# Paired PV matmuls on two banks, and MoE2's second weight factored one phase later

## The chip, the cores and the metric

The kernel runs on one core of a Trainium2 chip. The metric is the device time of one execution in microseconds (us), and lower is better. TensorE (PE in the profile) does the matmuls, VectorE (DVE) and ScalarE (ACT) read its results out of the eight PSUM banks, GpSimd (POOL) works on SBUF alone, and SyncE (SP) issues all DMAs from one queue.

## The reference

Causal attention with a decay, then two feed-forward layers. All inputs that matter for time are fixed in shape: 4 batches, 8 heads, 576 tokens of 64 values; 2304 tokens of 512 values afterwards, hidden width 2048.

```python
def _attn_ref(q, k, v, f):
    scores = scale * np.matmul(q, k.transpose(0, 1, 3, 2))
    cum = np.cumsum(np.log(np.clip(f, 0.0001, 1.0)), axis=-1)
    scores = np.where(causal, -1000000000.0, scores + cum[..., :, None] - cum[..., None, :])
    attn = np.exp(scores - np.max(scores, axis=-1, keepdims=True))
    attn = attn / (np.sum(attn, axis=-1, keepdims=True) + 1e-09)
    return np.matmul(attn, v)
def _moe_ref(x, w_in, w_out):      # 512 -> 2048 -> 512
    h = x @ w_in
    return (h * np.clip(h + 3.0, 0.0, 6.0) / 6.0) @ w_out
def _moe2_ref(x, w_in, w_out):     # 512 -> 2048 -> 512
    h = x @ w_in
    return (np.maximum(h, 0.0) + np.log1p(np.exp(-np.abs(h)))) @ w_out
```

## The kernel before

All matmuls of the two layers are done in three products of split operands (high part by high part, high by low, low by high), so each operand exists as a pair of tiles: ACT makes the high part, and DVE or GpSimd subtracts it from the value for the low part.

The work has four stages. **Attention** takes 16 head pairs one after the other: scores (`s_job`, L655), their minimum and exponent on DVE and ACT (L671, L680), transposes of the probabilities (`t_job`, L746, evicted at L771), the product with V (`pv_job`, L794) and its scaling (`norm`, L802). A head pair's PV consists of two jobs, idx 0 for queries 0 to 255 with 4 matmuls and idx 1 for queries 256 to 575 with 10. Each job is one planned step with a PSUM bank of its own, and the planner may place other matmuls between the two.

**MoE1** works on blocks of 512 tokens (the last has 256) and on 16 hidden tiles: `moe1_g1` (L1220) makes a hidden tile in a bank, ACT and DVE turn it into g (L1260, then L1262, which frees the bank), ACT and DVE split g (L1240, L1243), and `moe1_g2` (L1283) accumulates the output. MoE1 runs beside the attention; its last two blocks, interleaved, come after it.

**MoE2** uses Strassen's seven products, so each weight needs sums of its quarters before it is split. Its first phase is `step_a` (L1336, four token groups of eight hidden pairs each, three banks per step, evicted at L1351 and L1354 and stored after a softplus at L1379). Its second phase is `step_b` (L1433, nine token groups), for which `factors_g` loads the hidden values back, makes four sums (L1405) and three splits (L1412, L1416). `weights2` loads two raw weight tiles, makes four sums (L1029) and the splits (L1058 on ACT, L1061 on DVE or GpSimd). `weights2_in` uses it for the first weight. `weights2_out` uses it for pairs 0 to 6 of the second weight; each of its seven factors goes through a piece of the tile XO to DRAM and is loaded again at the end of the first phase (`load_wo`). In the kernel before, `weights2_out` is planned within MoE1's last blocks, with raw weights and pieces in XO and sums in XT, two tiles that are also MoE2's first factors of x.

A planner (`Work.order`) sets the order of every engine's queue. Each step has a due time `at` and, for each engine that may take it, a cost; the planner takes whatever can start first and breaks ties by due time. Steps made by `either` may go to DVE or to GpSimd, at the costs given there plus a penalty. A step that needs a new PSUM bank waits in the plan until one is free of those allowed to its kind, up to a cap (`capA` for attention, `capH` for hidden tiles). Engines then execute their queues in order. The numbers in `PLAN` scale due times, costs and caps.

## Time and profile before

| | |
|---|---|
| Median of 3 runs | 985.34 us (985.23 to 986.38) |
| The profiled execution | 985.61 us |
| Its span, first to last instruction | 983.8 us |
| PE busy | 958.2 us (97% of the span), 6140 matmuls |
| DVE, ACT, POOL busy | 644.4, 568.8, 170.1 us |
| Granted TensorE clock, mean | 0.996 |
| Attention with MoE1 | up to about 447 us |
| MoE1 alone | to about 610 us |
| MoE2, first and second phase | to about 795 us, to about 977 us |

The profile comes from one execution. Engines and their busy time stand in the table; in the views, a line such as L1262 is a line of the kernel before, `out<-in` are the tiles' names without buffer numbers, and an idle time is followed by the instruction that ended it. In the timeline the durations of pipelined instructions overlap, so what a matmul occupies is read from the distance between two starts.

### The profile page before, as it was taken

What the parts mean: (1) busy time and instruction counts of PE and PEld (TensorE: products, weight loads), DVE (VectorE), ACT (ScalarE), POOL (GpSimd) and SP (SyncE); (2) the same over time, 40 slices, a digit from 0 to 9 for tenths busy, and PEclk for the clock granted to TensorE, in tenths of its full rate; (3) what the DMA queues carried; (4) which work ended last, traced back from release to release, by engine and by line L of the source; (5) the groups of instructions that cost most, each with busy time, mean ns of one, the idle gap of its engine ahead of it and who ended that gap; (6) DMA issues with size and microseconds to landing.
All of it is one profiled execution on the core that took longest, in us unless ns stands there. A gap on an engine that the chain in (4) does not pass through costs nothing.

```text
span 983.8 us, 17265 instructions
## 1 busy us (share of the span) xinstructions
PE 958.2 (97%) x6140; PEld 831.1 (84%) x6140; DVE 644.4 (65%) x1359; ACT 568.8 (58%) x1245; POOL 170.1 (17%) x175
## 2 busy tenths in 40 slices
PE   8999999999999999999999999999999998999997
PEld 7676777777778777777888788999999998999997
DVE  8889767776565376664677675534443448888885
ACT  7888777776566476664445354656556543444441
POOL 2221222210000000000122210000000125545452
PEclk9999999999999999999999999999999999999999
DMA  6776576775774276645467633453426973454441
GB/s 137 184 170 172 151 181 174 189 198 144 206 179 124 53 206 191 190 132 163 150 204 236 200 96 108 161 160 109 157 97 234 391 272 108 138 146 126 129 129 66
DMA packets 196335, 161.29 MB, mean 164 GB/s; under 512 B 108972, under 2 KB 164684, under 8 KB 195352
## 3 DMA queue, kind: packets, MB, share of 16 engines
q1 hardware_dynamic: 196248, 160.19, 55.2%
q8 instruction: 48, 0.79, 0.3%
q14 instruction: 39, 0.32, 0.1%
HBM read 100.72 MB, written 53.52 MB: 157 GB/s over the span
## 4 chain that ended last, share of the span: by engine, by line
PE 80%; DVE 9%; ACT 4%; DMA 3%; issue 2%; SPq 1%; POOL 0%; DVEq 0%; ACTq 0%; POOLq 0%
PE bank L1336 17%; PE bank L1433 17%; PE bank L1220 17%; PE bank L1283 16%; PE bank L655 5%; PE bank L746 4%; PE bank L794 4%; DMA st<-in_moe_w_in_dram 1%; DVE GT L1262 1%; ACT pt L771 1%; DVE rW L1061 1%; DVE p L671 1%; DVE XO L1138 1%; ACT rW L1058 1%; ACT st L942 0%
## 5 line engine op out<-in xcount | busy, mean ns | idle before, releaser
L1220 PE MATMUL bank<-MX,W 128*128 128x512 f32 x768 | 222.8, 405 | 4.9 <-DVE GT L1262 4.6
L1283 PE MATMUL bank<-MX,W 128*128 128x512 f32 (+1 forms) x688 | 189.6, 382 | 0.2 <-ACT pt L771 0.2
L1220 PEld LDWEIGHTS bank<-MX,W 128*128 128x128 f32 x768 | 135.0, 190 | 29.9 <-DVE GT L1262 5.7
L1433 PE MATMUL bank<-rW,rW 128*128 128x256 f32 x1134 | 138.4, 283 | 2.0 <-DVE rW L1416 1.1
L1433 PEld LDWEIGHTS bank<-rW,rW 128*128 128x128 f32 x1134 | 136.8, 191 | 2.6 <-DVE rW L1416 1.5
L1283 PEld LDWEIGHTS bank<-MX,W 128*128 128x128 f32 x688 | 120.4, 189 | 20.6 <-ACT pt L771 0.4
L1336 PE MATMUL bank<-XO,rW 128*128 128x288 f32 x672 | 91.4, 297 | 1.7 <-ACT HY L1351 1.0
L1336 PEld LDWEIGHTS bank<-XO,rW 128*128 128x128 f32 x672 | 90.1, 188 | 2.4 <-ACT HY L1351 1.2
L1243 DVE TENSOR_TENSOR MX<-GT,MX 128x512 fp32r<-128x512 f32 (+1 forms) x69 | 46.7, 676 | 67.2 <-ACT MX L1240 66.3
L680 ACT ACTIVATE p<-p,stats 64x64 f32<-64x64 f32 (+4 forms) x130 | 72.1, 555 | 29.7 <-DVE stats L671 29.1
L1240 ACT ACTIVATE MX<-GT 128x512 fp32r<-128x512 f32 (+1 forms) x63 | 37.4, 596 | 83.5 <-PE bank L1283 81.7
L771 ACT ACTIVATE pt<-bank 128x448 f32<-128x448 f32 (+2 forms) x160 | 66.3, 432 | 33.1 <-PE bank L746 31.6
L1412 ACT ACTIVATE rW<-st 128x512 fp32r<-128x512 f32 x72 | 37.2, 519 | 79.8 <-PE bank L1433 56.5
L671 DVE CUSTOM_DVE_ANT_0 p<-bank,bar 64x64 f32<-64x64 f32 (+4 forms) x130 | 51.7, 423 | 43.4 <-PE bank L655 35.7
L1336 PE MATMUL bank<-MX,rW 128*128 128x288 f32 x480 | 70.6, 298 | 0.0
L1336 PEld LDWEIGHTS bank<-MX,rW 128*128 128x128 f32 x480 | 65.2, 188 | 0.5
L1260 ACT ACTIVATE GT<-bank,three 128x512 f32<-128x512 f32 (+1 forms) x80 | 51.0, 641 | 23.5 <-PE bank L1220 11.0
L1262 DVE SCALAR_TENSOR_TENSOR GT<-GT,bank 128x512 f32<-128x512 f32 (+1 forms) x80 | 50.0, 628 | 18.1 <-ACT GT L1260 17.5
L1416 POOL TENSOR_TENSOR rW<-st,rW 128x256 fp32r<-128x256 f32 (+1 forms) x34 | 40.3, 1186 | 114.0 <-ACT rW L1412 98.8
L746 PE MATMUL bank<-ident,p 128*128 128x128 f32 x390 | 58.1, 276 | 1.2 <-DVE xs L802 1.0
L746 PEld LDWEIGHTS bank<-ident,p 128*128 128x128 f32 x390 | 45.5, 141 | 16.1 <-ACT pt L771 3.8
L958 POOL TENSOR_TENSOR W<-st,W 128x512 fp32r<-128x512 f32 x24 | 32.0, 1336 | 133.8 <-ACT W L957 97.7
(186 smaller groups left out, 1678.0 us busy)
## 6 DMA issues: line engine op xcount, KB each, us to landing
st<-g_dram SPq DMA_DIRECT2D x36, 512.0 KB
st<-in_moe_w_in_dram SPq DMA_DIRECT2D x32, 512.0 KB
st<-in_moe_w_out_dram SPq DMA_DIRECT2D x32, 512.0 KB
wo_dram<-XO SPq DMA_DIRECT2D x49, 256.0 KB
g_dram<-HY SPq DMA_DIRECT2D x16, 576.0 KB
g_dram<-rBW SPq DMA_DIRECT2D x16, 576.0 KB
rW<-wo_dram SPq DMA_DIRECT2D x5, 1792.0 KB
wf_dram<-st SPq DMA_DIRECT2D x28, 256.0 KB
```

Source lines behind the costliest of these rows:

```text
L655: nc.tensor.matmul(acc[:m, o:o + c - a], qs[:, q0:q0 + m], ks[:, a:c], start=(n == 0 and ti == todo[-1][0]), stop=(n == len(ops) - 1), ski ...
L671: nc.vector.tensor_tensor_reduce(out=T["P"][par][ti][:r, a:c], in0=bank[bk.i][:r, o:o + c - a], in1=bar[:r, b0:b0 + c - a], op0=ALU.add, o ...
L680: nc.scalar.activation(out=pt, in_=pt, func=ACTF.Exp, scale=-1.0, bias=sv[:r, 0, ti:ti + 1], accum_out=sv[:r, 1, ti:ti + 1],)
L746: nc.tensor.transpose(acc[:, p0:p0 + P], T["P"][par][ti][:, k0:k0 + P], ident)
L771: e.activation(out=place(i, j, ks, a, c), in_=src(), func=ACTF.Copy)
L1220: nc.tensor.matmul(bank[bk.i][:, 0:n], w[:, c], x[:, c, 0:n], start=(c == 0 and p == 0), stop=(c == NC - 1 and p == 2))
L1243: op(("dve", dve(n), lambda: nc.vector.tensor_tensor(t(glt), g, t(ght).bitcast(F32), op=ALU.subtract)), r=[("g", i), ("gh", i3)], w=[("gl" ...
L1260: op(("act", act(n, True, 1), lambda: nc.scalar.activation(out=g, in_=bank[bk.i][:, 0:n], func=ACTF.Relu, bias=three)), r=["three"], banks ...
L1262: op(("dve", dve(n), lambda: nc.vector.scalar_tensor_tensor(out=g, in0=g, scalar=6.0, in1=bank[bk.i][:, 0:n], op0=ALU.min, op1=ALU.mult)), ...
L1283: nc.tensor.matmul(bank[b][:, o:o + n], w[:, c * P:(c + 1) * P], x, start=(ft == 0 and p == 0 and o == 0), stop=(ft == NF - 1 and p == 2), ...
L1336: nc.tensor.matmul(bank[bks[b].i][:, 0:HA], wa[u][:, c], xa[v][:, c], start=(nm in ("P1", "P2", "P5") and c == 0 and y == 0), stop=(c == 1 ...
L1433: nc.tensor.matmul(bank[bks[b].i][:, o * 256:(o + 1) * 256], ga[u], wa[v], start=(p == 0 and o == 0 and y == 0), stop=(p == NPR - 1 and y ...
```

## The change

1. `pv_job` makes one step of both PV jobs of a head pair: 14 matmuls in a row on two banks, and then two `norm` steps. The planner's bank search now looks for as many free banks as a step needs at once.
2. `weights2_out` moves into MoE2's first phase: pair k is planned beside step (t, p) with k = 3t + p/3 for p = 0, 3 and 6, until k = 6 at t = 2, p = 0. Its raw weights use the two staging tiles `st`, its pieces the tiles GT and rBL, four in all. The loads, sums, splits and the 49 stores move with it. XO and XT are then MoE2's alone.
3. In the planner, GpSimd as an alternative to DVE costs a penalty of 800 ns (`pq`); the penalties that DVE carried (`pv`, and 300 ns in `factors_g`) are gone.
4. The other numbers of `PLAN` are new, so the whole order is new. Among them `capH` goes from 3 to 2 and `capA` from 5 to 6.

Counted over the program, the instructions of PE, SP and ACT are the same but for one on ACT; DVE has 1439 in place of 1361 and GpSimd 101 in place of 180. In MoE2's second phase DVE takes 24 more splits of 256 columns, 8 more of 512 and 20 more sums of 256, and GpSimd keeps 27 sums and 2 splits. Of the MoE1 matmuls (1920 in the program), 1062 stand ahead of the last PV before the change and 852 after it.

```diff
+    pq=800,
...
-    capH=3,
-    capA=5,
+    capH=2,
+    capA=6,
...
-                    for b in o.banks:
-                        if b.i is None:
-                            if b.kind in caps and used.get(b.kind, 0) >= caps[b.kind]:
-                                s = 1e18
-                                break
-                            t = min((bank_free[i] for i in b.allowed if owner[i] is None and (held[i] == 0 or b.kind not in caps)), default=1e18)
-                            s = max(s, t)
+                    new = [b for b in o.banks if b.i is None]
+                    if new:
+                        b = new[0]
+                        t = sorted(bank_free[i] for i in b.allowed if owner[i] is None and (held[i] == 0 or b.kind not in caps))
+                        if b.kind in caps and used.get(b.kind, 0) + len(new) > caps[b.kind] or len(t) < len(new):
+                            continue
+                        s = max(s, t[len(new) - 1])
...
-    def pv_job(b, hp, idx, at):
+    def pv_job(b, hp, at):
         z = (b * HP + hp) % 2
         wk.mark = ()
-        bk = Bank(att_banks, "a")
-        a, c = V_JOBS[idx]
+        bks = [Bank(att_banks, "a") for _ in V_JOBS]
...
             for j, ta, tcc in jobs:
-                if ta < c and tcc > a:
-                    rd += [("PT", i, j, ta - KCUT[j][0]) for i in range(2)]
-        todo = [(i, j, max(a, KCUT[j][0]) - KCUT[j][0]) for j in V_ORDER[idx] for i in range(2)]
+                rd += [("PT", i, j, ta - KCUT[j][0]) for i in range(2)]
+        todo = [(x, i, j, max(a, KCUT[j][0]) - KCUT[j][0]) for x, (a, c) in enumerate(V_JOBS) for j in V_ORDER[x] for i in range(2)]
...
         def go():
-            acc = bank[bk.i]
-            for n, (i, j, s) in enumerate(todo):
+            for n, (x, i, j, s) in enumerate(todo):
+                a, c = V_JOBS[x]
                 k0 = KCUT[j][0]
-                nc.tensor.matmul(acc[i * D:i * D + D, s + k0 - a:c - a], T["vr"][z][:, j, i], place(i, j, slice(0, P), s, c - k0),
-                                 start=(n < 2), stop=(n >= len(todo) - 2), skip_group_check=True)
-
-        op(("pe", sum(0.833 * (c - KCUT[j][0] - s) + 3 for _, j, s in todo) + 190, go), r=rd, w=[bk], banks=[bk], at=at, name=f"PV{idx}")
+                nc.tensor.matmul(bank[bks[x].i][i * D:i * D + D, s + k0 - a:c - a], T["vr"][z][:, j, i], place(i, j, slice(0, P), s, c - k0),
+                                 start=(j == V_ORDER[x][0]), stop=(j == V_ORDER[x][-1]), skip_group_check=True)
+
+        op(("pe", sum(0.833 * (V_JOBS[x][1] - KCUT[j][0] - s) + 3 for x, _, j, s in todo) + 290, go), r=rd, w=bks, banks=bks, at=at, name="PV")
...
-        op(("dve", dve(c - a), lambda: nc.vector.tensor_tensor(X()[:, a:c], bank[bk.i][:, 0:c - a], ivb[:, a:c], op=ALU.mult)),
-           r=["ivb"], banks=[bk], w=[("xs", z, idx)], at=at, name="norm")
-        if idx == 0:
-            return
+        for x, (a, c) in enumerate(V_JOBS):
+            op(("dve", dve(c - a), lambda x=x, a=a, c=c: nc.vector.tensor_tensor(X()[:, a:c], bank[bks[x].i][:, 0:c - a], ivb[:, a:c], op=ALU.mult)),
+               r=["ivb"], banks=[bks[x]], w=[("xs", z, x)], at=at, name="norm")
...
-                    elif what == "v" and prev and prev[2]:
-                        pv_job(*prev[:2], idx, at - K["tsp"])
+                    elif what == "v" and idx and prev and prev[2]:
+                        pv_job(*prev[:2], at - K["tsp"])
...
-    def either(n, fn, late=K["pv"]):
-
-        return [("dve", dve(n), lambda: fn(nc.vector), late), ("pool", 2.8 * n + 60, lambda: fn(nc.gpsimd))]
+    def either(n, fn, late=0.0):
+
+        return [("dve", dve(n), lambda: fn(nc.vector), late), ("pool", 2.8 * n + 60, lambda: fn(nc.gpsimd), K["pq"])]
...
-        own = i0 >= 8
-
-        def raw(i):
-            return BIG["XO"][:, (i - 8) * NC * P:(i - 7) * NC * P].bitcast(F32)
...
         def x(i, e, j, n=1):
-            if own:
-                return (BIG["XT"][:, i * 2 * h:] if e else raw(i0 + i))[:, j * h:(j + n) * h]
             return words(i0 + i)[:, e, j * h:(j + n) * h]
...
-    NPC = (7 * XW - 4 * NC * P) // (4 * P)
+    NPC = 4
 
     def piece(i):
-        return BIG["XO"][:, 4 * NC * P + i * 4 * P:][:, 0:4 * P].rearrange("p (s f) -> p s f", s=2)
+        return (BIG["rBL"] if i % 2 else GT)[:, i // 2 * 4 * P:][:, 0:4 * P].bitcast(F32R).rearrange("p (s f) -> p s f", s=2)
...
-    def weights2_out(p, at, i0):
+    def weights2_out(p, at, pace):
...
-        weights2(1, p, at, parts, i0, [("pace1", (3 * p + 1) // 2)])
+        weights2(1, p, at, parts, 0, [pace])
...
-            op(either(2 * P, go, 300), r=[("stage", i)] + [("C", i, y) for y in (u, v) if isinstance(y, int)], w=[("C", i, x)], at=at, name="gS")
+            op(either(2 * P, go), r=[("stage", i)] + [("C", i, y) for y in (u, v) if isinstance(y, int)], w=[("C", i, x)], at=at, name="gS")
...
-            op(either(n, lo, 300), r=rd + [("gf", i, z0, 0)], w=[("gf", i, z0, 1)], at=at + 1, name="gfl")
+            op(either(n, lo), r=rd + [("gf", i, z0, 0)], w=[("gf", i, z0, 1)], at=at + 1, name="gfl")
...
-        if p < NPR - 1:
-            weights2_out(p, moe_at(NB - 2, 2 * p + 1) + 14, 8 + p % 2 * 2)
...
-    freed([("stage", 8 + i) for i in range(4)] + [("piece", i) for i in range(NPC)], [("xf", 0, f) for f in AT[2]])
-    freed([("up", 8), ("up", 9)], [("xt", 0), ("xt", 1)])
+    freed([(x, i) for x in ("stage", "up") for i in (4, 5)], [("piece", i) for i in range(NPC)])
...
             step_a(t, p)
+            k = t * 3 + p // 3
+            if p % 3 == 0 and k < NPR - 1:
+                weights2_out(k, ma_at(t, p) + 2, ("pace", t, p))
...
-    freed([("stage", 4), ("up", 4)], [("C", 1, x) for x in range(4)])
-    freed([("stage", 5), ("up", 5)], [("u", x) for x in range(3)])
+    freed([("piece", 0), ("piece", 2)], [("C", 1, x) for x in range(4)])
+    freed([("piece", 1), ("piece", 3)], [("u", x) for x in range(3)])
```

PE in the attention, at one head pair: the end of PV job 0 (L794), MoE1's first matmul (L1220), and the start of PV job 1. Before:

```order
L794 MATMUL bank_76<-pt_171,vr 64x128
L794 MATMUL bank_76<-pt_175,vr 64x128
L1220 MATMUL bank_72<-MX,W_1334 128x512 x3
L794 MATMUL bank_76<-pt_170,vr 64x320
L794 MATMUL bank_76<-pt_174,vr 64x320
```

The same engine at a head pair after the change (L792 is the PV line there):

```order
L792 MATMUL bank_75<-pt_171,vr_179 64x128
L792 MATMUL bank_75<-pt_175,vr_179 64x128
L792 MATMUL bank_76<-pt_170,vr_179 64x320
L792 MATMUL bank_76<-pt_174,vr_179 64x320
L792 MATMUL bank_76<-pt_171,vr_179 64x320
```

The two jobs now follow each other on two banks. Before the change other matmuls stood between them at 10 of the 16 head pairs; now at none.

DVE in MoE1's last blocks, from one g (L1262) to the next; XT and XO are `weights2_out`'s sums and pieces, st belongs to `weights2_in`. Before:

```order
L1262 SCALAR_TENSOR_TENSOR GT<-GT,bank_72 128x256
L1029 TENSOR_TENSOR XT<-XO 128x256
L1029 TENSOR_TENSOR XT<-XO,XT 128x256
L1243 TENSOR_TENSOR SB<-GT,SB 128x512
L1029 TENSOR_TENSOR st_180<-st_181 128x256
L1029 TENSOR_TENSOR st_181<-st_180,st_181 128x256
L1029 TENSOR_TENSOR st_180<-st_180 128x256
L1061 TENSOR_TENSOR XO<-XT,XO 128x256
L1262 SCALAR_TENSOR_TENSOR GT<-GT,bank_71 128x512
```

The same engine in these blocks after the change (L1252 is g, L1233 the split of g, L1019 the sums):

```order
L1252 SCALAR_TENSOR_TENSOR GT<-GT,bank_71 128x256
L1019 TENSOR_TENSOR st_180<-st_181 128x256
L1233 TENSOR_TENSOR SB<-GT,SB 128x512
L1019 TENSOR_TENSOR st_181<-st_180,st_181 128x256
L1019 TENSOR_TENSOR st_180<-st_180 128x256
L1019 TENSOR_TENSOR st_181<-st_180 128x256
L1252 SCALAR_TENSOR_TENSOR GT<-GT,bank_72 128x512
```

The XT and XO steps have left the stretch between two g. GpSimd, which has 29 instructions between 460 and 619 us before the change, has one of `weights2_in` left there.

DVE in MoE2's first phase; L1354 adds a product out of a bank, L1138 and L1143 make the factors of x. Before:

```order
L1354 TENSOR_TENSOR HY<-HY,bank_70 128x288
L1138 TENSOR_TENSOR MX<-XT,MX 128x576
L1354 TENSOR_TENSOR HY<-HY,bank_69 128x288 x2
L1138 TENSOR_TENSOR SB<-XT,SB 128x576
L1143 TENSOR_TENSOR XT<-MX,XT 128x576
L1354 TENSOR_TENSOR rBW<-rBW,bank_70 128x288
```

After the change (L1344 is the addition out of a bank, L1051 a split, GT and rBL the pieces):

```order
L1128 TENSOR_TENSOR SB<-XT,SB 128x576
L1344 TENSOR_TENSOR rBW<-rBW,bank_70 128x288
L1133 TENSOR_TENSOR XT<-MX,XT 128x576
L1344 TENSOR_TENSOR HY<-HY,bank_69 128x288
L1128 TENSOR_TENSOR MX<-XT,MX 128x576
L1051 TENSOR_TENSOR GT<-st_180,GT 128x256
L1051 TENSOR_TENSOR rBL<-st_180,rBL 128x256
L1344 TENSOR_TENSOR rBW<-rBW,bank_71 128x288
```

The splits of the second weight now stand among the additions that empty the banks.

## Rows read from the trace of the kernel before

**Rows 1.** The page: busy time, share of the span, instructions of each engine.

```profile
PE 958.2 (97%) x6140; PEld 831.1 (84%) x6140; DVE 644.4 (65%) x1359; ACT 568.8 (58%) x1245; POOL 170.1 (17%) x175
```

**Rows 2.** Stretches: length, busy PE, PEld, DVE, ACT, POOL (count); clock, DMA share, GB/s.

```profile
60.00:110.00 50.00, 45.37 (x272) 36.08 (x272) 44.37 (x109) 42.38 (x104) 10.32 (x9) 0.97 0.71 176
110.00:212.00 102.00, 100.29 (x561) 77.55 (x560) 73.80 (x167) 77.00 (x174) 26.71 (x20) 1.00 0.67 172
212.00:410.00 198.00, 197.69 (x1049) 153.39 (x1048) 117.14 (x294) 121.64 (x277) 0.00 (x0) 1.00 0.60 163
...
460.00:619.00 159.00, 153.44 (x859) 132.61 (x858) 107.97 (x205) 77.20 (x164) 28.38 (x29) 0.99 0.52 167
...
660.00:795.00 135.00, 135.00 (x1009) 134.37 (x1008) 54.62 (x106) 75.30 (x162) 4.48 (x5) 1.00 0.57 211
...
840.00:930.00 90.00, 90.00 (x754) 89.78 (x754) 76.92 (x117) 36.27 (x58) 44.83 (x41) 1.00 0.46 135
```

**Rows 3.** PE's waits, 460 to 619 us: total us, times, longest us.

```profile
PE bank L1220 <- DVE GT L1262: 4.6, 4, 2.0
```

**Rows 4.** Timeline of PE, 541 to 551 us: start, us, instruction, idle before.

```profile
545.07 0.97 PE L1220 MATMUL bank<-MX,W 128*128 128x512 f32 x3 [2.05 <-DVE GT L1262]
...
546.96 1.49 PE L1220 MATMUL bank<-MX,W 128*128 128x512 f32 x3
```

**Rows 5.** The stretch behind that wait, columns as in Rows 2.

```profile
546.00:549.00 3.00, 3.00 (x11) 2.49 (x10) 0.36 (x2) 0.00 (x0) 0.00 (x0) 0.52 1.04 343
```

**Rows 6.** Timeline of DVE, 536 to 547 us.

```profile
539.35 0.42 DVE L1029 TENSOR_TENSOR XT<-XO 128x256 f32<-128x256 f32 x1
...
543.48 0.94 DVE L1061 TENSOR_TENSOR XO<-XT,XO 128x256 fp32r<-128x256 f32 x1
544.34 0.68 DVE L1262 SCALAR_TENSOR_TENSOR GT<-GT,bank 128x512 f32<-128x512 f32 x1
```

**Rows 7.** Timeline of POOL, 500 to 600 us.

```profile
542.36 1.78 POOL L1061 TENSOR_TENSOR XO<-XO 128x256 fp32r<-128x256 f32 x2
```

**Rows 8.** Timeline of PE, 254 to 261 us: a PV whose jobs stand apart.

```profile
254.70 0.87 PE L794 MATMUL bank<-pt,vr 128*64 128x256 f32 x8
255.50 0.97 PE L1220 MATMUL bank<-MX,W 128*128 128x512 f32 x3
256.31 0.63 PE L1283 MATMUL bank<-MX,W 128*128 128x512 f32 x2
256.77 0.39 PE L1283 MATMUL bank<-MX,BW 128*128 128x512 f32 x1
257.01 0.86 PE L1220 MATMUL bank<-MX,W 128*128 128x512 f32 x3
257.80 2.27 PE L794 MATMUL bank<-pt,vr 128*64 128x320 f32 x20
260.01 0.97 PE L1220 MATMUL bank<-MX,W 128*128 128x512 f32 x3
```

**Rows 9.** Timeline of PE, 118 to 124 us: a PV whose jobs stand together.

```profile
120.00 2.92 PE L794 MATMUL bank<-pt,vr 128*64 128x256 f32 x28
122.86 0.96 PE L1220 MATMUL bank<-MX,W 128*128 128x512 f32 x3
```

**Rows 10.** PE's waits from 795 us on.

```profile
PE bank L1433 <- DVE rW L1416: 2.0, 3, 0.9
```

**Rows 11.** Timeline of DVE, 820 to 824 us.

```profile
821.35 2.31 DVE L1416 TENSOR_TENSOR rW<-GT,rW 128x1024 fp32r<-128x1024 f32 x1
```

**Rows 12.** DVE groups from 795 us on: count | busy us, mean ns | idle before.

```profile
L1416 DVE TENSOR_TENSOR rW<-XT,rW 128x1024 fp32r<-128x1024 f32 x17 | 21.3, 1255 | 4.4 <-ACT rW L1412 4.4
...
L1405 DVE TENSOR_TENSOR XT<-st 128x256 f32<-128x256 f32 x16 | 14.6, 914 | 0.0
...
L1405 DVE TENSOR_TENSOR GT<-st,GT 128x256 f32<-128x256 f32 x15 | 6.4, 425 | 0.5
```

**Rows 13.** PE's waits, 15 to 110 us.

```profile
PE bank L746 <- DVE xs L802: 1.0, 1, 1.0
```

More of the change, by code (lines that the diff above doesn't have):

```diff
@@ L49 @@
     NZ=6,
[L50 to L56 removed]
+    pq=800,
+    pc=2608.6,
+    pp=1453.02,
+    pg=489.39,
+    iva=-0.35,
+    cA=0.89,
+    bend=[1.43, 0.96, 0.78, 0.4],
+    gap2=58.61,
     nwarm=18,
     NS=4,
[L59 to L81 removed]
+    b0=45.34,
+    T0=62.83,
+    P1=3.82,
+    P2=2.2,
+    P3=2.23,
+    SA=4.11,
+    SB=2.5,
+    evb=-0.26,
+    splag=0.49,
+    g2lag=8.81,
+    cv=14.72,
+    cvw=53.52,
+    ldw=171.48,
+    gap=23.47,
+    gap3=35.7,
+    tsp=-4,
+    xat=221.48,
+    xl=3.5,
+    rel=58.51,
+    wfrom=8.79,
+    lv0=9.04,
+    lq1=15.07,
     decst=30,
@@ L997, in weights2 @@
     def weights2(o, p, at, parts, i0, pace=()):
-        own = i0 >= 8
-        def raw(i):
-            return BIG["XO"][:, (i - 8) * NC * P:(i - 7) * NC * P].bitcast(F32)
         for z in range(2):
             i, ft = i0 + z, 2 * p + z
-            if not own and (o, ft) in late2:
+            if (o, ft) in late2:
                 raw_weights(i, 1, o, ft, at, True)
@@ L1010, in load @@
             def load(i=i, ft=ft):
-                dst = raw(i) if own else words(i)[:, 0]
+                dst = words(i)[:, 0]
                 if wide:
@@ L1030, in sums @@
             op(either(h, go), r=r + list(pace), w=w, at=at - 2, name=name)
-        s0, s1, u0, u1 = ((x, 8 + i if own and x == "up" else i0 + i) for x in ("stage", "up") for i in range(2))
+        s0, s1, u0, u1 = ((x, i0 + i) for x in ("stage", "up") for i in range(2))
         X11, X12, X21, X22 = (0, 0, 0), (0, 0, 1), (1, 0, 0), (1, 0, 1)
```

31 lines of the change are left out of this document (1 added, 30 removed).

## The prediction

> **What bounds the kernel now.** I read the page first, then the busy time by stretch, then PE's waits in the stretches that are not full, and at each wait the timelines of the engine that ended it.
>
> PE is busy for 958.2 of 983.8 us [rows 1], so the order can give back only waits, and the little that PE loses between unlike matmuls. The stretches say where the waits are [rows 2]: 4.63 us of 50 from 60 to 110 us, 1.71 of 102 from 110 to 212, 0.31 of 198 from 212 to 410, 5.56 of 159 from 460 to 619 (MoE1 alone and the start of MoE2), none from 660 to 795 and none from 840 to 930.
>
> In the stretch from 460 to 619 one wait counts: PE waits four times, 4.6 us in all, for g on DVE (L1262), which frees the hidden tile's bank [rows 3]. The longest is 2.05 us [rows 4]. Behind it the granted clock is 0.52 for 3 us [rows 5], which is the 1.2 GHz level for nearly all of them: three matmuls there take 1.49 us from the first start to the last end [rows 4], where 0.86 is usual [rows 8]. The cause is on DVE. Just ahead of that g stands a row of sums and splits for the two weights, and each takes about 0.95 us where the same size took 0.42 a little earlier [rows 6]. At that time GpSimd runs splits of the same kind [rows 7]. So DVE is late for two reasons: it has other work in its queue, and that work is slow while GpSimd reads SBUF beside it.
>
> **The change part by part.** The sum is made against the profiled execution, 985.6 us with a span of 983.8; the median of the three runs is 985.3.
>
> PV in one group. Where the jobs stand apart, job 0 occupies 0.80 us (254.70 to 255.50) and job 1 2.21 us (257.80 to 260.01), 3.01 in all [rows 8]; together they take 2.86 us (120.00 to 122.86) [rows 9], so 0.15 is saved. A switch into PV and out of it costs as well. Three MoE1 matmuls take 0.70 us among their like (256.31 to 257.01), 0.79 ahead of a PV (257.01 to 257.80) and 0.81 behind one (255.50 to 256.31) [rows 8]: 0.09 and 0.11 more, once less per pair. That is 0.35 for each of the 10 pairs that stand apart: **-3.4** with some loss where the neighbour is not MoE1, between -1.5 and -3.5.
>
> The second weight out of MoE1's last blocks. Seven pairs with four sums and seven splits each are 77 steps of 256 columns for DVE or GpSimd, and 49 copies on ACT. DVE was busy for 107.97 us of that stretch and GpSimd for 28.38 [rows 2]; at 0.42 us a step [rows 6] at least 20 us leave DVE, nearly all of GpSimd's work leaves, and what stays on DVE is no longer slowed. I take 4.1 of the 4.6 us [rows 3] as gone, and the late clock with them: 0.48 of 3.0 us [rows 5] is 1.4. What is late next is the first weight's sums, which still stand between two g, but four of them at 0.42 are 1.7 us, less than the 2.8 us for which the 12 matmuls of the next hidden tile keep PE busy (0.70 for three [rows 8]). **-5.5** together; if the first weight and the late conversions still hold g up, between 0 and -6.0.
>
> The same work in MoE2's first phase. DVE is busy for 54.62 us of 135 there, ACT for 75.30, and PE is full [rows 2]. 77 steps at 0.42 [rows 6] are 32 us more for DVE, and 49 copies, if they take as long, 21 for ACT, over about 100 us. I cost that at nothing: a step uses three of eight banks, so PE is more than a step ahead of the additions that empty them, and the longest row of the new work that stands ahead of such an addition is four splits, 1.7 us. If that cover were gone and every pair's row were waited for, seven times 1.7, it would cost 11.8. SP's queue also gets 14 loads and 49 stores; a store waits for its split, and queued behind it are the stores of hidden values and the loads of x. Both have two sets of buffers, so a delay reaches PE only after a whole step.
>
> The attention. 210 of MoE1's matmuls, which stood ahead of the last PV, now stand behind it. At 0.70 us for three [rows 8] that is 49 us by which the attention gets denser. Taken from the stretch of 198 us, whose DVE was busy for 117.14 [rows 2], and with 12 us of MoE1's own DVE work gone (8.7 hidden tiles of 24 matmuls, each with a g of 0.68 [rows 6] and a split of that size), DVE has 105 us in 149: 70%, about as from 110 to 212 us (73.80 of 102, 72%) [rows 2]. Waiting there was 1.7%, which on 149 us is 2.5 against 0.31 before: **+2.2**. The bounds are 0 and the rate from 60 to 110 us, 9.3% (DVE 44.37 of 50) [rows 2], which would be +13.5. I take the row whose density fits. The first 110 us are rearranged too, and nothing in the rows says to which side; I leave them at nothing, and their 4.63 us of waits [rows 2] are a reason for width.
>
> Less GpSimd in MoE2's second phase. DVE takes 24 splits and 20 sums of 256 columns and 8 splits of 512: 44 times 0.42 and 8 times 0.68 [rows 6] are 23.9 us over 180. It was busy for 76.92 of 90 us [rows 2]. In exchange its own steps get shorter: a sum took 0.914 us in the group that runs beside GpSimd and 0.425 in one that doesn't [rows 12]. 47 such sums and the splits give back about as much, so the phase stays full of PE. At its start PE waited three times for a split, 2.0 us [rows 10]; one of them followed a split that took 2.31 us beside GpSimd [rows 11] where its like took 1.255 in the mean [rows 12]. I take **-1.0**, between 0 and -2.0.
>
> Sum: 985.6 - 3.4 - 5.5 + 2.2 - 1.0 = 977.9, rounded to **978.0 us**.
>
> **The rivals.**
>
> *The gain at MoE1's end does not come.* Each g still waits behind the first weight's sums and the late conversions, and PE falls to the low clock once more. For it: their order is much as before. Against it: the slow steps were slow beside GpSimd [rows 6, 7], which is nearly empty there now. Time: 985.6 - 3.4 + 2.2 - 1.0 = 983.4.
>
> *The attention is crowded (slower).* PE waits in the denser attention at the rate of 60 to 110 us: 977.9 + 13.5 - 2.2 = 989.2. It decides from a waiting share of about 8% on: the gains are 9.9 us, and those and 2.0 more on 149 us are 8%. For it: `capH` is 2, so PE has less MoE1 work to fall back on. Against it: 1.7% was enough at equal density.
>
> *Two banks at once (slower).* PE once waited 1.0 us for the scaling of a PV [rows 13]. Both banks of a pair are now freed only after the whole group, one scaling after the other. If each of the 16 pairs paid this, the time would be 977.9 + 16 = 993.9. Against it: the longest such wait among all pairs was that one, and six pairs already stood together. The Trainium skill, on the page Trainium Kernel Development and Optimization (Best Practices), says to mind PSUM pressure, because TensorE tiling speeds up compute but not the emptying of PSUM; by that rule a longer tiled group moves the cost to the banks, which is this rival. The trace agrees with it only at that one wait.
>
> *DVE becomes the bound of the second phase (slower).* Without shorter steps DVE would have 76.92 + 12.0 in 90 us, and the 29 steps left to GpSimd at 0.49 us each would add 14 over 180, 7 in 90: 96 of 90. It decides where DVE's sum passes 90. Over 180 us that is 12.2 us: 990.1. Against it: rows 12.
>
> *Better than forecast.* The attention's waits do not grow and the second phase starts without a wait for a split: 977.9 - 2.2 - 1.0 = 974.7.
>
> **How the numbers follow.** A measurement of this kernel can tell about 0.2%, 2 us, from no change. Chances: the forecast 0.52, better than forecast 0.14, no gain at MoE1's end 0.14, crowded attention 0.10, DVE as the bound 0.06, two banks 0.04. Faster by over 0.2% (under 983.4) are the first two and half of the third: 0.73. The slower three hold 0.20; milder forms of them and the other half of the third end within 0.2%: 0.09 for the same, 0.18 for slower. The range takes in the first three cases with the bounds of their terms, that is 0.8. The lower bounds of all terms give 985.6 - 3.5 - 6.0 + 0 - 2.0 = 974.1, and a us of the first 110 us makes it 973; no gain at MoE1's end with PV at its upper bound gives 985.6 - 1.5 + 2.2 - 0 = 986.3, so 986.
>
> **What the new profile would show.** Right: no PE wait for g between MoE1's last blocks, no stretch of low clock there, sums of 256 columns on DVE at 0.42 us; 28 PV records in a row at each head pair; PE full in MoE2's first phase with DVE near 60%; a second phase without waits after its start. Wrong: waits of PE for PV's scaling or for scores in the attention's second half, PE waiting for the additions in MoE2's first phase, or DVE without idle time in the second. Waits or a low clock in the first 110 us would move the time either way without a step of mine.

## The result and the profile after

The changed kernel is **slower**: 995.67 us in the median of 4 runs (993.97 to 996.71) against 985.74 for the kernel before in the median of 4, a ratio of 1.0099 with a 95% interval of 1.0081 to 1.0116. The prediction was 978.0 with a range up to 986. The profiled execution took 996.71 us, with a span of 994.9 against 983.8, so 11.1 us of span have to be found.

The page's first part of the changed kernel (as in [rows 1]), then its stretches with the columns of [rows 2]:

```profile
PE 960.5 (97%) x6140; PEld 829.0 (83%) x6140; DVE 644.4 (65%) x1437; ACT 571.2 (57%) x1246; POOL 90.9 (9%) x96
```

```profile
60.00:110.00 50.00, 42.95 (x245) 31.43 (x244) 45.80 (x109) 41.20 (x97) 12.44 (x10) 0.97 0.69 170
110.00:212.00 102.00, 97.32 (x543) 75.08 (x541) 73.07 (x169) 79.02 (x177) 26.41 (x20) 1.00 0.65 168
212.00:410.00 198.00, 196.28 (x1110) 150.33 (x1111) 119.20 (x320) 125.25 (x304) 0.00 (x0) 1.00 0.54 144
460.00:619.00 159.00, 158.56 (x874) 136.40 (x873) 80.01 (x147) 66.33 (x122) 1.49 (x1) 1.00 0.21 65
660.00:795.00 135.00, 131.53 (x965) 129.01 (x964) 74.21 (x166) 85.51 (x194) 2.91 (x2) 1.00 0.81 280
840.00:930.00 90.00, 88.56 (x741) 88.14 (x740) 76.02 (x142) 37.53 (x60) 14.55 (x14) 1.00 0.43 129
```

Against [rows 2], PE stands idle longer in every stretch but 460 to 619, where 5.56 us of idle time became 0.44. From 660 to 795 us, full before, 3.47 us are idle.

Both kernels run 6140 matmuls of the same shapes, so the stages can be compared by their **loss**: a stage's time less the sum of its matmuls' usual durations (0.234 us for 512 columns, 0.133 for 288 and so on), added up from all PE records of a profiled execution. Only differences from before are used. The stages are the first 110 us, the rest of the attention up to the last PV, MoE1 alone, and MoE2's two phases. From before to after the loss changed by +7.3, +5.8, -6.2, +5.7 and -1.4 us, together the 11.1, up to rounding. Where the granted clock falls to half, the matmuls take longer than usual, and that counts as loss too.

### The profile page after: what moved, and what is told of

Read it like the earlier page. It is cut to its first block, busy times and chain, and to the rows that moved or that the text cites. A ratio compares the mean times of both kernels' runs of the same rounds, so it can differ in the third digit from the quotient of the medians.

```text
span 994.9 us, 17232 instructions
## 1 busy us (share of the span) xinstructions
PE 960.5 (97%) x6140; PEld 829.0 (83%) x6140; DVE 644.4 (65%) x1437; ACT 571.2 (57%) x1246; POOL 90.9 (9%) x96
## 4 chain that ended last, share of the span: by engine, by line
PE 67%; DMA 10%; DVE 9%; ACT 8%; issue 3%; SPq 3%; POOL 0%; DVEq 0%; ACTq 0%
PE bank L1273 15%; PE bank L1210 15%; PE bank L1423 14%; PE bank L1326 13%; PE bank L746 3%; PE bank L655 3%; PE bank L792 3%; DMA st<-in_moe_w_in_dram 2%; DMA st<-g_dram 2%; DMA st<-in_moe_w_out_dram 2%; ACT pt L771 2%; ACT p L680 1%; DVE st L942 1%; DMA st<-wf_dram 1%; DMA ivb<-inv_dram 1%
## 5 line engine op out<-in xcount | busy, mean ns | idle before, releaser
L1233 DVE TENSOR_TENSOR MX<-GT,MX 128x512 fp32r<-128x512 f32 (+1 forms) x69 | 46.2, 671 | 74.3 <-ACT MX L1230 73.4
L671 DVE CUSTOM_DVE_ANT_0 p<-bank,bar 64x64 f32<-64x64 f32 (+4 forms) x130 | 51.6, 422 | 44.7 <-PE bank L655 44.2
L771 ACT ACTIVATE pt<-bank 128x320 f32<-128x320 f32 (+2 forms) x160 | 66.0, 431 | 21.7 <-PE bank L746 20.1
L1230 ACT ACTIVATE MX<-GT 128x512 fp32r<-128x512 f32 (+1 forms) x58 | 34.3, 592 | 75.7 <-PE bank L1273 74.0
L1252 DVE SCALAR_TENSOR_TENSOR GT<-GT,bank 128x512 f32<-128x512 f32 (+1 forms) x80 | 50.0, 628 | 30.9 <-ACT GT L1250 30.7
L939 ACT ACTIVATE st<-st 128x512 f32<-128x512 f32 x64 | 43.3, 679 | 17.8 <-DMA st<-in_moe_w_in_dram 10.7
L942 DVE SCALAR_TENSOR_TENSOR st<-st 128x512 uint32<-128x512 uint32 x64 | 47.7, 745 | 8.6 <-ACT st L939 7.4
```

Source lines behind the costliest of these rows:

```text
L671: nc.vector.tensor_tensor_reduce(out=T["P"][par][ti][:r, a:c], in0=bank[bk.i][:r, o:o + c - a], in1=bar[:r, b0:b0 + c - a], op0=ALU.add, o ...
L771: e.activation(out=place(i, j, ks, a, c), in_=src(), func=ACTF.Copy)
L942: op(("dve", dve(n), lambda: nc.vector.scalar_tensor_tensor(out=words(i)[:, 0].bitcast(U32) if dense else low(), in0=up(), scalar=3, in1=l ...
L1233: op(("dve", dve(n), lambda: nc.vector.tensor_tensor(t(glt), g, t(ght).bitcast(F32), op=ALU.subtract)), r=[("g", i), ("gh", i3)], w=[("gl" ...
L1252: op(("dve", dve(n), lambda: nc.vector.scalar_tensor_tensor(out=g, in0=g, scalar=6.0, in1=bank[bk.i][:, 0:n], op0=ALU.min, op1=ALU.mult)), ...
```

## The experiments

Each row of the table is one kernel with its median, its ratio to the kernel before with the interval (before was timed beside each group of runs; its medians lie between 985.66 and 986.84 us), the loss by stage less that of before, and the mean granted clock of the first 110 us, which was 0.98 before. Losses and clock come from one profiled execution each, which can lie some us off the median (e1's by 3.7).

The fourth row is a null: another dealing of nearly the same work moves a stage by up to 2 us, and that execution as a whole by 3. A single execution brings its own difference too, by the clock. e3 and e8 have the same order on every engine up to 627 us, and yet their first 110 us differ by 3.4 us of loss, at clocks of 0.97 and 1.00. A hundredth of clock over 110 us is worth about 1.1 us, if PE is busy (an estimate: a hundredth of 110). In MoE1 alone only the execution of before has a stretch of low clock, the one of [rows 5]; e4, e5, e10 and e11, which leave that stage's work as it was, show -1.3 to -1.9 there, about what it is worth (3.4 us at half the clock, 1.7).

| kernel | median us | ratio (95%) | first 110 | attention | MoE1 alone | phase 1 | phase 2 | clock, first 110 |
|---|---|---|---|---|---|---|---|---|
| changed | 995.67 | 1.0099 (1.0081-1.0116) | +7.3 | +5.8 | -6.2 | +5.7 | -1.4 | 0.98 |
| e1 changed code, old numbers | 996.27 | 1.0103 (1.0086-1.0119) | +4.9 | +14.0 | -6.4 | +4.3 | -2.5 | 0.97 |
| e2 old code, new numbers | 998.15 | 1.0129 (1.0114-1.0144) | +11.2 | +5.9 | -3.3 | -0.2 | 0.0 | 0.94 |
| e4 null | 985.29 | 0.9996 (0.9985-1.0007) | -1.9 | +1.4 | -1.3 | +0.2 | -1.2 | 1.00 |
| e5 PV group alone | 998.65 | 1.0134 (1.0110-1.0158) | +6.2 | +10.1 | -1.9 | +0.2 | 0.0 | 0.95 |
| e6 moved factors alone | 990.51 | 1.0052 (1.0033-1.0070) | +0.5 | +0.2 | -2.8 | +6.7 | 0.0 | 0.98 |
| e7 less GpSimd alone | 978.32 | 0.9927 (0.9906-0.9948) | -0.3 | +0.3 | -5.2 | -0.8 | -3.3 | 0.98 |
| e10 late first half | 992.13 | 1.0064 (1.0044-1.0085) | +6.6 | +0.4 | -1.3 | +0.1 | +0.5 | 0.97 |
| e11 two banks, jobs apart | 993.08 | 1.0063 (1.0042-1.0084) | -0.8 | +9.2 | -1.6 | +0.3 | -1.0 | 1.00 |
| e12 e7 and moved factors | 982.52 | 0.9954 (0.9938-0.9969) | +1.3 | +0.3 | -6.3 | +4.4 | -2.9 | 0.97 |
| e16 e7, still less GpSimd | 976.92 | 0.9902 (0.9880-0.9923) | -0.4 | +0.5 | -6.6 | -0.1 | -3.6 | 1.00 |
| e3 changed, 7 numbers back | 989.97 | 1.0042 (1.0026-1.0057) | +4.4 | +3.5 | -6.3 | +6.9 | -3.0 | 0.97 |
| e9 changed, PV apart | 1005.28 | 1.0181 (1.0152-1.0211) | +14.3 | +6.0 | -6.7 | +7.1 | -1.2 | 0.91 |
| e17 e3, PV apart | 990.13 | 1.0045 (1.0030-1.0060) | +4.5 | +2.0 | -6.5 | +5.8 | -2.5 | 1.00 |
| e8 e3, factors ranked later | 988.63 | 1.0031 (1.0016-1.0045) | +1.0 | +5.8 | -6.2 | +5.5 | -2.0 | 1.00 |
| e18 changed, no factor loads | 992.11 | 1.0068 (1.0051-1.0085) | +5.8 | +5.6 | -6.3 | +2.7 | -2.7 | 1.00 |
| e13 e3, limits back | 996.23 | 1.0112 (1.0082-1.0142) | +4.3 | +4.2 | -5.9 | +7.5 | -1.8 | 0.98 |
| e14 e3, pace back | 990.94 | 1.0044 (1.0026-1.0062) | +5.6 | +1.5 | -7.2 | +8.5 | -2.4 | 0.97 |
| e15 e3, ranks back | 994.39 | 1.0081 (1.0053-1.0110) | +4.1 | +7.3 | -7.0 | +6.6 | -2.7 | 0.97 |

### Code or numbers

The first theory came from rows of the changed kernel's head. Its timeline, 27.5 to 33 us:

```profile
27.67 0.77 DVE L576 STREAM_TRANSPOSE KF<-kr 64x576 f32<-64x576 f32 x1
...
31.77 0.69 ACT L939 ACTIVATE st<-st 128x512 f32<-128x512 f32 x1 [3.22 <-DMA st<-in_moe_w_in_dram]
...
31.84 0.43 DVE L941 TENSOR_SCALAR st<-st 128x512 uint32<-128x512 uint32 x1 [3.40 <-DMA st<-in_moe_w_in_dram]
...
32.18 0.45 DVE L671 CUSTOM_DVE_ANT_0 p4b<-bank,bar 128x288 f32<-128x288 f32 x1
...
32.70 0.75 PE L655 MATMUL bank<-KF,QF 97*128 97x288 f32 x2 [1.67 <-DVE stats L671]
```

ACT and DVE take their work in order. Both stand over 3 us at a weight's conversion (L939, L941) whose load has not landed, and the softmax minimum (L671) for which PE waits is queued behind. The new numbers put these conversions there; before, neither engine waits for such a load in its first 110 us. PE's waits for the minimum's result (stats) in that time, before first, then in the changed kernel:

```profile
PE bank L655 <- DVE stats L671: 0.5, 1, 0.5
```

```profile
PE bank L655 <- DVE stats L671: 2.3, 3, 1.7
PE bank L700 <- DVE stats L671: 2.2, 1, 2.2
```

So e1 takes all numbers back, e2 puts the new ones alone into the old code, and e3 puts back seven of them:

```diff
-    wfrom=8.79, ldw=171.48, cvw=53.52, cv=14.72, lv0=9.04, lq1=15.07, rel=58.51,
+    wfrom=14.07, ldw=55.43, cvw=17.59, cv=19.18, lv0=16.35, lq1=28.4, rel=23.68,
```

e4 changes `T0=50.96` to `T0=51.2` in the kernel before.

> The changed code (PV of a head pair as one group on two banks, the second weight's factors in MoE2's first phase, fewer GpSimd offers) with the planner's numbers of the kernel before; only the numbers go back. Theory H (head): the new numbers pull the load and conversion of MoE1's weights into batch 0's attention, and ScalarE and VectorE, which take their work in order, stand there waiting for a weight's load while the softmax is queued behind: the head of after (some 14 us later at the last PV) goes, the rest of after stays: PV -1.9, end of MoE1 -5.8, MoE2's first phase +5, start of its second -2: 980 to 984 us, last PV near 445 or a little below. Rival S (structure): a PV that takes two banks at once holds up the scores: attention stays slow with the old numbers too, 990 us or more. Rival R (any new deal of the planner's order loses): 990 us or more, with waits spread over all stages.

> The code of the kernel before with the new numbers alone. Theory H: the loss of the first 110 us is there without any of the changed code: PE waits over 60 ns before 110 us at 12 to 14 us against 6.4 of before, 993 to 1001 us in all, with MoE1's end as before or worse. Rival S: the numbers cost nothing, 983 to 988 us. Rival R: slower than before too, but not in the first 110 us above all.

> The changed kernel with seven of its numbers put back, those that say when MoE1's weights and the first heads are loaded and converted (wfrom, ldw, cvw, cv, rel, lv0, lq1). Theory H: 982 to 987 us; rows in which ScalarE and VectorE wait at the conversion for a weight's load before 110 us go away. Rival (the loss comes of the ends set for each batch and MoE1's pace, not of the weights): 993 to 998 us.

> The kernel before with one number nudged (T0 50.96 to 51.20, the start of MoE1 in the plan), which deals some 13% of the rows anew and changes nothing in what is done. Theories H and S: 984 to 988 us, so a new deal alone is worth 2 us at most. Rival R: 990 us or more.

The null stayed at 985.29, so a small new dealing doesn't lose by itself; as it deals only some 13% of the rows anew, theory R is weakened and not refuted. e2 (998.15) agrees with H in time and in the head (+11.2), and e3 gives 5.7 us back, less than expected. But H's rows don't follow the loss. In the first 110 us ACT and DVE together wait 9.7 us for weight loads in the changed kernel and 3.5 in e3, where H had them gone; yet in e17 below they wait 8.3 us and the loss is +4.5, and in e15 0.3 us with +4.1. That these numbers cost time is shown; that the wait for a load is how they do it is shown for the one wait of 1.67 us above. And e1 is as slow as the changed kernel, so the code has a fault of its own, in another place: +14.0 in the attention (of an execution 3.7 us slower than e1's median).

### The parts alone

e5 to e7 put one part each into the kernel before: the hunks of `pv_job` with the search for banks; those of `weights2` and `weights2_out`; and the surcharge on GpSimd:

```diff
-        return [("dve", dve(n), lambda: fn(nc.vector), late), ("pool", 2.8 * n + 60, lambda: fn(nc.gpsimd))]
+        return [("dve", dve(n), lambda: fn(nc.vector), late), ("pool", 2.8 * n + 60, lambda: fn(nc.gpsimd), K["pq"])]
```

> The kernel before with the PV of a head pair as one group on two banks (and the planner's search for two banks), nothing else. As the prediction had it, with what the changed kernel measured: a pair saves 0.19 us x 16, so 980 to 984 us. Rival S (two banks at once, and a PV that waits for the last key tile of both halves, hold up the head and the scores): the first 110 us lose 3 to 6 us and a later batch some more, 988 to 996 us.

> The kernel before with the second weight's factors moved into MoE2's first phase, nothing else. Theory A: the end of MoE1 gets 4 to 6 us shorter (waits 4.6 us to under 1, one stretch of low clock gone), the first phase 4 to 7 us longer by additions that wait behind the factors' rows on VectorE, the second phase 0 to 2 us shorter: 982 to 987 us, attention unchanged. Rival (the first phase's loss came of the new numbers or of less GpSimd): the first phase within 1.5 us of before, 978 to 982 us.

> The kernel before with the offers to GpSimd priced 800 ns higher (and VectorE's 300 ns surcharge at the second phase's factors gone), nothing else. If this is a cause of its own: the second phase loses 2 us or more, 988 us or above. If it is none: 983 to 987 us, with GpSimd busy at about half of before.

The PV group alone costs 12.5 us (998.65 against 986.12), the moved factors 4.4, and less GpSimd **gains 7.8**, which no theory expected. They add: 12.5 + 4.4 - 7.8 = 9.1, and e1, which holds all three, measured 10.6 (996.27 against 985.66).

What e7 changes in the rows, the page first, then 460 to 619 us as in [rows 2], PE's waits up to 605 us as in [rows 3], and sums of 256 columns from 795 us on as in [rows 12]:

```profile
PE 954.2 (98%) x6140; PEld 829.2 (85%) x6140; DVE 642.5 (66%) x1434; ACT 569.0 (58%) x1245; POOL 85.9 (9%) x100
```

```profile
460.00:619.00 159.00, 156.65 (x898) 136.47 (x897) 109.32 (x228) 80.58 (x171) 11.07 (x11) 1.00 0.53 172
```

```profile
PE bank L1220 <- DVE GT L1262: 1.3, 3, 0.9
```

```profile
L1405 DVE TENSOR_TENSOR GT<-st 128x256 f32<-128x256 f32 x29 | 11.0, 419 | 1.0 <-DMA st<-g_dram 1.0
L1405 DVE TENSOR_TENSOR XT<-st 128x256 f32<-128x256 f32 x25 | 9.9, 418 | 1.6 <-DMA st<-g_dram 1.6
```

DVE has 75 instructions more than before and is busy 1.9 us less in all: its own steps got shorter by about what was added. With the factors still at MoE1's end, the waits for g fall from 4.6 to 1.3 us and the stretch of low clock is gone (1.00 against 0.99). The null, with 5.0 us of such waits, has no low clock there either, so some 1.7 of the 5.2 us that this stage gains can't be put down to e7's edit.

### Why the PV group costs

The group does two things: its first half may start only when the last tiles of P are copied, and two banks are held until two scalings are done. e10 does the first alone, in the kernel before, e11 the second:

```diff
-                if ta < c and tcc > a:
+                if True:
```

```diff
-        bk = Bank(att_banks, "a")
+        if idx == 0:
+            both[:] = [Bank(att_banks, "a") for _ in V_JOBS]
+        bk = both[idx]
...
-r=rd, w=[bk], banks=[bk], at=at, name=f"PV{idx}")
+r=rd, w=[bk], banks=list(both) if idx == 0 else [bk], at=at, name=f"PV{idx}")
```

> The kernel before with PV in its two jobs and one bank each, but the first job made to wait for all tiles of P, as the group does. Theory L (the group costs because its first half may no longer fill PE while the last tiles of P are still copied): 993 to 999 us, as the PV group alone (998.65), with a wait near 355 us. Theory K (it costs because a pair holds two banks until two scalings are done): 984 to 988 us.

> The kernel before with PV in its two jobs, each ready when it was, but both banks taken at the first. Theory K: 993 us or more, with PE's waits for a bank that a scaling holds. Theory L: 984 to 988 us.

Both cost, in different places, and together as much as the group: 6.6 in the first 110 us by e10 and 9.2 later by e11, against 6.2 and 10.1 in e5. Neither L nor K was right alone.

e10's waits up to 110 us, then its timeline at the longest:

```profile
PE bank L655 <- DVE xs L802: 3.3, 2, 1.7
...
PE bank L746 <- DVE xs L802: 1.2, 1, 1.2
```

```profile
67.72 0.82 DVE L802 TENSOR_TENSOR xs<-bank,ivb 128x256 f32<-128x256 f32 x2
...
68.20 0.40 PE L655 MATMUL bank<-KA,QA 128*128 128x288 f32 x1 [1.73 <-DVE xs L802]
```

Before, PE waited once for a scaling, 1.0 us [rows 13]. With both halves late, both scalings come in one piece, and scores and transposes wait for their banks: 4.5 us in three waits. Ahead of the longest DVE is busy with other work. Ahead of the other two it stands idle itself, for 1.84 us at 32 us and for 2.86 us at 47 us, the second time because the load of the factors that the scaling multiplies by (`ivb`) has not landed.

e11 at the border between two blocks of MoE1:

```profile
342.95 2.27 PE L798 MATMUL bank<-pt,vr 128*64 128x320 f32 x20
...
349.19 0.50 SPq L821 DMA_DIRECT2D x_dram<-xs  x1
...
350.05 0.55 PE L746 MATMUL bank<-ident,p 128*128 128x128 f32 x3 [1.36 <-DVE stats L671]
...
352.07 0.47 PE L746 MATMUL bank<-ident,p 128*128 128x128 f32 x1 [1.47 <-ACT p L680]
...
355.52 0.50 SPq L1186 DMA_DIRECT2D MX<-x_dram  x1
```

```profile
350.00:358.00 8.00, 5.92 (x28) 4.30 (x30) 5.75 (x10) 6.10 (x14) 0.00 (x0) 0.57 0.89 238
```

The twelfth pair's PV ends at 345.2 us here and at 334.4 before. Its output goes through memory to be the next block's tokens: stored at 349.19 and asked back at 355.52 (336.76 and 339.07 before), with loads of the next heads between on SP's queue. MoE1 runs out of work at matmul 795 of 1920, from 342.6 to 359.7 us. Alone, the chain of the softmax leaves PE idle, and it runs at a clock of 0.57 in the stretch shown. Of e11's +9.2 in the attention nearly all falls between 342 and 362 us (9.4 us of loss, 1.0 in the same stretch before); up to there the loss is within 1 us of before's. So the PV comes late by the order: the plan puts other work ahead of it. That it does so because it looks for two free banks follows from the edit; no row shows it. Before, the same matmul followed its predecessor at once (347.3, 347.5). The same hole stands in e5 (352.6 to 367.2) and e1 (355.2 to 370.2). The Trainium skill says, on the page Trainium Kernel Development and Optimization (Best Practices), that tiling TensorE doesn't speed up the emptying of PSUM. e10's 4.5 us of waits for scalings fit that; e11's larger price is another one, a late PV that starves the next stage.

### The group in the changed kernel

e9 puts PV's two jobs back into the changed kernel, e17 does that with the seven numbers back.

> The changed kernel with PV put back into two jobs, one bank each; its numbers and everything else stay. Theory P (the PV group is a cause of its own in the changed kernel too, as it was alone, +12.6 us): the attention loses most of what it lost, 982 to 988 us. Rival N (with the new numbers the PV group is paid for, and the loss of the attention is the numbers' own, as they lost 12.5 us in the old code): 993 to 999 us.

> The changed kernel with the seven head numbers put back and PV in its two jobs again. Theory L (the late first half is what the head still loses): the first 110 us lose 4 to 6 us less, the PV itself 2 us more: 985 to 988 us against 990.0. Rival (the other new numbers lose without the group, as when PV alone was put apart, 1005 us): 995 to 1002 us.

Here the group's sign turns: with the new numbers it gains 9.6 us (1005.28 against 995.67); with the seven numbers back it makes no difference (989.97, 990.13). So P falls, and so does the thought of e17 that the late first half is what the head still loses. The seven numbers cost 15.2 us with PV apart and 5.7 with the group. Most of the first is clock: in the first 110 us PE is idle for 13.75 us in e9 and for 12.79 in e17, nearly the same, but the clock is 0.91 against 1.00, which by the estimate above is 9.9 us of a difference in loss of 9.8. It isn't one odd execution: over the whole program e9's four runs have mean clocks of 0.988 to 0.994, e17's of 0.999 to 1.000. Most of the group's 9.6 us lies there too (0.91 against 0.98). e9's head has two waits over 2 us and a low clock behind each; PE's timeline and the stretches:

```profile
89.15 3.23 PE L1213 MATMUL bank<-MX,W 128*128 128x512 f32 x6 [2.43 <-ACT MX L809]
...
94.77 0.30 PE L700 MATMUL bank<-ident,bar 128*128 128x128 f32 x1 [2.39 <-DVE bar L697]
```

```profile
88.00:92.00 4.00, 2.85 (x6) 1.78 (x6) 3.90 (x7) 3.95 (x8) 1.04 (x1) 0.62 0.81 170
...
96.00:100.00 4.00, 3.70 (x14) 2.86 (x15) 3.84 (x10) 3.93 (x9) 0.00 (x0) 0.50 0.74 130
```

What the group saves of PE's own time is there. The changed kernel's timeline of PE at a PV:

```profile
386.22 0.86 PE L1210 MATMUL bank<-MX,W 128*128 128x512 f32 x3
387.01 2.93 PE L792 MATMUL bank<-pt,vr 128*64 128x256 f32 x28
389.86 0.97 PE L1210 MATMUL bank<-MX,W 128*128 128x512 f32 x3
390.67 0.93 PE L746 MATMUL bank<-ident,p 128*128 128x128 f32 x7
```

Three MoE1 matmuls take 0.79 us ahead of the PV and 0.81 behind it, as the prediction read in [rows 8]. Each run of PV that is gone saves these 0.09 and 0.11 at its neighbours.

### MoE2's first phase

The changed kernel's timeline at one of its waits, and what waits there from 619 to 806 us:

```profile
664.15 0.43 DVE L1019 TENSOR_TENSOR st<-st 128x256 f32<-128x256 f32 x1 [1.45 <-DMA st<-wf_dram]
...
664.50 1.21 DVE L1019 TENSOR_TENSOR st<-st,st 128x256 f32<-128x256 f32 x3
665.63 0.45 DVE L1344 TENSOR_TENSOR rBW<-rBW,bank 128x288 f32<-128x288 f32 x1
...
666.13 1.06 PE L1326 MATMUL bank<-XO,rW 128*128 128x288 f32 x6 [0.80 <-DVE rBW L1344]
```

```profile
DVE st L1019 <- DMA st<-wf_dram: 4.5, 5, 1.5
...
PE bank L1326 <- DVE rBW L1344: 2.7, 4, 1.1
...
PE bank L1326 <- DVE HY L1344: 1.1, 3, 0.5
```

A sum waits 1.45 us for its load, three more follow, then the addition, then PE. e8 gives the factors a later rank; e18 leaves the loads out and keeps every engine's order.

```diff
-                weights2_out(k, ma_at(t, p) + 2, ("pace", t, p))
+                weights2_out(k, ma_at(t, p) + 14, ("pace", t, p))
```

```diff
             def load(i=i, ft=ft):
+                if pace:
+                    return
```

> The changed kernel with the seven head numbers put back (as in the run with those numbers) and the factors' rank in the first phase put 12 us later (ma_at + 14 in place of + 2), so that additions and evictions that are ready go ahead of them. Theory A: the waits of the first phase fall from 6.2 us to 3 or less and the phase by 3 to 5 us: 984 to 987 us, against 990.0. Rival (rank is not it: the engines hold the slot while one long row runs, or the factors' total work is too much): 988.5 to 991 us.

> The changed kernel, the same order on every engine, without the loads of the second weight for the factors made in MoE2's first phase (left out: 12 to 14 loads of 256 KB, so the factors come of what lies in the buffer). Theory W (VectorE stands at a sum that waits for its load, with additions behind it): the waits of the first phase fall from 4.8 us to 3 or less, 992 to 994 us. Rival (the rows' own time and the 1.6 us steps beside GpSimd do it): the phase within 1 us of the changed kernel, 995 to 997 us.

The rank takes PE's waits for additions in this phase from 5.2 us in e3 to 2.9, but the loss by only 1.4 (6.9 to 5.5, with a stretch of low clock at e8's longest wait) and the time by 1.3, within what a new dealing does: not settled. Without the loads the phase loses 3.0 us less (5.7 to 2.7). Its waits, 617 to 801 us:

```profile
PE bank L1328 <- DVE HY L1346: 1.2, 3, 0.6
...
PE bank L1328 <- DVE rBW L1346: 0.8, 1, 0.8
```

So about half of the loss comes with the loads, which DVE waits for in its order; the medians differ by 3.6 us. The other 2.7 us stay: the rows' own time and the stores are left there and aren't taken apart. (The first 110 us of e18 lost 1.5 us less in the same order: the clock there was 1.00 in place of 0.98.)

e12 joins the moved factors, ranked later, to e7:

> The kernel before with the cheaper half of the change: fewer GpSimd offers and the second weight's factors in MoE2's first phase (ranked 12 us later there), old numbers, PV apart. If the parts add: less GpSimd alone -7.5 us, the moved factors +3 to +5 on top because MoE1's end is already free of most waits: 981 to 984 us. Rival (the moved factors pay once GpSimd no longer slows VectorE in the first phase): 975 to 978 us, better than less GpSimd alone.

The parts add, as far as the intervals tell (0.9954 against e7's 0.9927, and they just overlap): some 4 us slower than e7. MoE1's end gains 1.1 from the move once GpSimd is quiet, and phase 1 pays 5.2.

### What the other numbers do, and the best kernel

Three more groups of numbers went back on top of e3: `capA`, `capH` (e13); b0, T0, P1 to P3, SA, cA and the batch ends (e14); pc, pp, pg, iva, the lags, evb, tsp, xat, xl (e15). e16 is e7 with `pq=2000`.

> The changed kernel with the seven head numbers and the limits of banks put back (attention at most 5 instead of 6, hidden tiles at most 3 instead of 2). Theory B (with two hidden tiles PE has too little of MoE1 to fall back on while the attention's chain runs): the attention loses 3 us or more less, 983 to 987 us against 990.0. Rival: 988.5 to 992 us.

> The changed kernel with the seven head numbers and the ends of batches and MoE1's pace put back (b0, T0, P1, P2, P3, SA, cA, bend, gap, gap2, gap3). Theory D (the denser attention, ended 36 us earlier, is what loses): the last PV near 446 us again and the attention's loss 4 us or more less: 982 to 986 us. Rival (with these, the wait near 350 us at the border of two batches comes back, as with all numbers of before): 992 to 998 us.

> The changed kernel with the seven head numbers and the ranks and prices put back (pc, pp, pg, iva, splag, g2lag, evb, tsp, xat, xl). If these are what the head still loses: 984 to 987 us. If not: 988.5 to 993 us. Nothing speaks for one of them beforehand.

> The kernel before with less GpSimd alone, at a price of 2000 ns instead of 800. If each step beside GpSimd slows VectorE's own (0.42 to about 0.95 us), what is left on it is worth something too: 974 to 977.5 us against 978.3. If VectorE now has too much in the second phase: 979 us or more.

None of the three groups is the cause by itself: e14 is as e3, e13 is slower, and e15 probably. The 4 to 6 us that the first 110 us still lose in all of them, in e3 and in e17, are left open; part is clock, as e8 loses 1.0 there in e3's own order. e16 takes **976.92 us** (0.9902, 0.9880 to 0.9923), faster than both kernels; that it beats e7 (0.9906 to 0.9948) is likely, not shown.

## Why the prediction was wrong

- **The first 110 us, left at nothing: the step that failed most.** They cost 7.3 us; the range held 1 us for them, on the fast side. The clock was the same as before (0.98), so it is waiting: PE is idle for 15.23 us there, 8.93 before, and 4.8 of the 6.3 more are waits for the softmax minimum on DVE (5.3 us in five waits, 0.5 in one before). One of these waits, 1.67 us, has a load of weights ahead of it, another, 2.23 us, DVE's steps beside a GpSimd split (last section); how the rest came about is open. The new numbers bring it: e2 has it without the changed code, and putting seven back gave 5.7 us of the time. How that divides between the head and the attention isn't settled, as e3 and e8 show. "Nothing in the rows says to which side" was no reason for zero.
- **The attention, +2.2: mis-sized.** It lost 5.8 us, some 2.3 of PV's saving taken off (six of the ten pairs stand behind 110 us), so near +8, inside the bound of +13.5 and close to the rival "crowded attention". From 212 to 410 us PE's idle time is 1.72 us, no more than the 2.5 that the term held; what it left out is 110 to 212 us, from which it took its rate: 1.71 us became 4.68. Density isn't what decides: e17, whose last PV is at 402.9 us, loses 2.0, e14, at 454.7, 1.5, and e13, at 454.6, 4.2. The cause stays open.
- **PV, -3.4: right for PE's own time, with a price left out.** What PE spends at its PV runs beyond the columns, without waits, fell from 4.9 to 3.0 us (26 runs became 16), so -1.9, and the neighbours of ten runs fewer give up to 2.0 more. But the group has a second price that the sum didn't hold: a later first half and a bank held longer, 12.5 us in the old order (e5). In the changed kernel that price doesn't show: the group gains there or makes no difference. The rival "two banks at once", at 993.9, had a nearby mechanism and its size for e5; in the changed kernel PE waits for a scaling in the first 110 us only 0.9 us, so it isn't that rival which came true there.
- **MoE1's end, -5.5: right** (-6.2). The waits for g are 0.4 us and no low clock follows. But the move isn't needed for most of it: less GpSimd alone gives -5.2, the move alone -2.8, and some 1.7 of each of these three is the low clock of the one execution of before. That part, 1.4 in the forecast, came by luck: the null keeps the waits and has no low clock.
- **MoE2's first phase, at nothing: wrong** (+5.7). "PE is more than a step ahead of the additions" was the faulty step. Three of eight banks per step doesn't mean that. `CHAIN` adds P6, P7 and P4 onto P1 in one bank and P3 onto P5 in another, so PE needs that bank read within the same step: at 666.13 us P3 waits for the addition that reads P5 out of its bank. The move alone costs about as much (e6, +6.7). I also counted four splits as the longest row and left out the wait for a load ahead of it. The bound, +11.8, held.
- **The second phase, -1.0: right** (-1.4). New there are 1.4 us in two waits of PE for an addition (L1451 in the changed kernel). In e7, which leaves the factors where they were, the phase gives -3.3: less GpSimd was worth more than I put down.
- **The sum.** MoE1's end and the second phase made -7.6, forecast at -6.5. The first 110 us, the attention and MoE2's first phase, put at 0, +2.2 and 0, made +18.8 with PV's saving in it, in place of -1.2.

## What to carry to other kernels

Try the parts of a change alone: here one of three gained 0.7% and the other two and the re-tuned numbers hid it. Before work is moved beside a full engine, look for the rows that wait for a DMA in an in-order queue and for what is queued behind them; free banks are no cover where products accumulate in one bank. A step that holds a resource longer is paid where the filler work runs out, so look for the border at which another stage needs its output. Before a stage's loss is read from one execution each, compare their granted clocks.
